# A gate load in two halves, and the first gate unit begun on the first of them

## The chip, the cores and the metric

The kernel runs on one core of one Trainium2 chip. The metric is the device time of one execution in microseconds (us). All runs that are compared here are, with the kernel before, run in the same rounds on the same chip. Engines are named as in the profile: PE is TensorE (matmuls), PEld its weight loads, DVE VectorE, ACT ScalarE, POOL GpSimd, SP the engine that issues most loads.

## The reference, cut to what matters

```python
xn = _layernorm(x, axis=-1, eps=1e-5)                # x: 2048 x 512, bf16
return x + _A_ref(xn, w_r, w_i) + _B_ref(xn, w_gate, w_up, w_down)
# _B_ref: h = gelu(xn @ w_gate) * (xn @ w_up);  h @ w_down      (w_gate, w_up: 512 x 1792)
# _A_ref: a 2-D real FFT of xn, a product with w_r + i w_i, and the inverse FFT
```

## The kernel before

The rows of x are taken as 16 "columns" of 128 rows. Columns 0 and 1 are normalised first and transposed by PE. Then gate and up products start while the rest of the weights comes in, in small units (a unit is the product of some columns with some weight columns). Everything is one fixed order of instructions per engine, made by a small scheduler from estimated times.

The parts that the change touches:

```python
    pin(load_x(0, 1))
    pin(load_x(1, 1))
    idx_t = pc.tile([P, 3], I32, name="idx_t")
    nc.sync.dma_start(out=idx_t[:], in_=...)          # 1.5 KB, used after 40 us
    load_w(Wg_sb, 0, 512)                             # 512 KB: all four contraction blocks e of gate columns 0..511
    load_w(Wu_sb, 0, 512)                             # 512 KB: the first up load
    load_x(2, 2)
    for e in range(0, NE, 2):
        load_w(Wg_sb, 512, 1024, e=slice(e, e + 2))
    load_w(Wu_sb, 512, 1024)                          # the second up load
    load_x(4, 4)
    load_w(Wg_sb, 1024, DF)
    load_w(Wu_sb, 1024, DF)
    load_x(8, 2)
    load_x(10, 2)
    # ... (cut)

    def spin_on():                                    # fillers that keep PE busy
        for k in range(11):
            nc.tensor.matmul(sp_ps[:, :P], lhsT=spin[:], rhs=x_t[:, 0, :P], start=True, stop=True)

        # ... (cut) first unit: column 0, gate columns 0..511
        if k == 0:
            g = add("PE", occ / 4, lambda: mm_part(0, 1), [xT_op[0, 0]], key=1000, acq=("G",), t_min=WG_LAND[0])
            between["t", 0].deps.append(g)            # column 1's transposes come behind this quarter
            g = add("PE", occ / 4, lambda: mm_part(1, 2), [g, between["t", 1]], key=1000.1)
            g = add("PE", occ / 2, lambda: mm_part(2, NE), [xT_op[0], g], key=1000.2, lat=occ / 2 + 0.3)
```

All these loads are issued by SP, one after the other. From the ninth load on, each waits for the landing of the one eight places before.

## Time and profile before

| kernel before | us |
|---|---|
| median of three runs (178.33 to 178.76) | 178.74 |
| span of the profiled run | 176.9 |
| first gate matmul | 6.66 |
| first up load: issued, landed, wanted by PE | 2.65, 8.05, 8.63 |
| second up load: issued, landed, wanted by PE | 4.89, 11.99, 12.69 |

"Landed" is the last of the 16 increments of a load's semaphore in the trace, "wanted" the first weight load that reads it. SP's timeline (start, length of the issuing instruction):

```profile
2.18 0.43 SPq L277 DMA_DIRECT2D Wg_sb<-in_B_w_gate_dram  x1
2.65 0.51 SPq L277 DMA_DIRECT2D Wu_sb<-in_B_w_up_dram  x1
```

And the table of stretches of one microsecond; its last two columns are the busy share of the DMA engines and GB/s:

```profile
4.00:5.00 1.00, 1.00 (x12) 0.91 (x9) 0.94 (x4) 0.30 (x1) 0.00 (x0) 1.00 0.92 280
5.00:6.00 1.00, 0.73 (x9) 0.38 (x8) 0.93 (x5) 0.29 (x1) 0.00 (x0) 1.00 1.10 378
6.00:7.00 1.00, 0.97 (x18) 0.80 (x16) 0.67 (x4) 0.00 (x0) 0.00 (x0) 1.00 1.07 378
```

From 5 to 7 us the DMA engines are busy throughout.

### The profile page before, as it was taken

The numbers are of one execution on the slowest core, as the hardware profiler recorded it, in microseconds if no ns is written. First come the engines' busy times: TensorE is split into PE (matmuls) and PEld (weight loads), VectorE is DVE, ScalarE is ACT, GpSimd is POOL, SyncE is SP. The second block draws the span as 40 slices with busy tenths as digits, with TensorE's granted clock in tenths as the row PEclk, the third lists the DMA queues.
The fourth block names the chain that finished last, engine by engine and source line by source line (L and its number), as shares of the span: only waits on it lengthen the run. The fifth ranks groups of instructions, "written<-read, shape, count | busy, mean of one in ns | idle before, by whom it ended". The sixth has DMA issues, their size and how long they took to land.

```text
span 176.9 us, 3143 instructions
## 1 busy us (share of the span) xinstructions
PE 172.8 (98%) x1150; PEld 96.9 (55%) x1150; DVE 115.9 (66%) x255; ACT 96.0 (54%) x171; POOL 17.2 (10%) x38
## 2 busy tenths in 40 slices
PE   7999999999999999999999999999999999999993
PEld 7798845455545554555555455454445445444463
DVE  2588999987434599979899999643516325345333
ACT  3452489799736988898899965362112111211200
POOL 1020340506760000000000000000000000000000
DMA  3999999233717802211201510200122221221212
GB/s 99 323 387 377 371 199 151 60 64 71 246 41 238 299 0 59 59 30 35 59 19 42 152 47 15 59 0 4 59 89 89 77 75 60 89 88 60 82 40 59
DMA packets 21743, 19.35 MB, mean 109 GB/s; under 512 B 8480, under 2 KB 20000, under 8 KB 21728
## 3 DMA queue, kind: packets, MB, share of 16 engines
q1 hardware_dynamic: 21312, 17.84, 36.4%
q0 software_dynamic: 416, 1.32, 2.6%
q8 instruction: 9, 0.15, 0.4%
q14 instruction: 6, 0.05, 0.1%
HBM read 13.38 MB, written 2.10 MB: 87 GB/s over the span
## 4 chain that ended last, share of the span: by engine, by line
PE 95%; DVE 2%; DMA 1%; issue 0%
PE u_ps L494 27%; PE y_ps L829 27%; PE g_ps L494 25%; PE g_ps L502 2%; PE bp L589 2%; PE yp L780 2%; PE gp L750 2%; PE dp L647 2%; PE y_ps L833 2%; PE ep L656 2%; DMA x_t<-in_A_x_dram 1%; DVE stats L339 1%; PE tp L351 1%; DVE xn L345 0%; DVE xnT L354 0%; DVE y_sb L836 0%
## 5 line engine op out<-in xcount | busy, mean ns | idle before, releaser
L494 PE MATMUL u_ps<-xnT,Wu_sb 128*128 128x512 bf16 (+2 forms) x272 | 57.1, 341 | 0.0
L494 PE MATMUL g_ps<-xnT,Wg_sb 128*128 128x512 bf16 (+1 forms) x224 | 53.3, 364 | 0.0
L829 PE MATMUL y_ps<-Wd_sb,hT 128*128 128x512 bf16 (+2 forms) x252 | 51.1, 355 | 0.0
L512 DVE TENSOR_TENSOR hT<-u_ps,ge 128x512 bf16<-128x512 f32 x56 | 38.4, 688 | 18.1 <-PE u_ps L494 16.5
L507 ACT ACTIVATE ge<-g_ps 128x512 bf16<-128x512 f32 x56 | 33.5, 601 | 22.3 <-PE g_ps L494 18.3
L494 PEld LDWEIGHTS <-Wu_sb 128*128 128x128 bf16 x272 | 24.8, 98 | 20.7
L829 PEld LDWEIGHTS <-hT 128*128 128x128 bf16 x252 | 23.2, 98 | 22.4
L494 PEld LDWEIGHTS <-Wg_sb 128*128 128x128 bf16 x224 | 21.5, 98 | 20.5
L786 ACT CAST yf<-yp 128x512 bf16<-128x512 f32 x16 | 9.3, 586 | 40.5 <-PE yp L780 40.5
L836 DVE TENSOR_TENSOR y_sb<-y_ps,y_sb 128x512 bf16<-128x512 f32 (+2 forms) x18 | 11.1, 632 | 30.0 <-PE y_ps L833 30.0
L661 ACT CAST E<-ep 64x512 bf16<-64x512 f32 x32 | 18.5, 579 | 1.4 <-PE ep L656 1.0
L339 DVE BATCH_NORM_STATS2 stats<-x_t 128x6 f32<-128x512 bf16 x16 | 10.4, 674 | 3.9 <-DMA x_t<-in_A_x_dram 3.9
L456 ACT ACTIVATE xn<-x_t,nb,rstd 128x512 bf16<-128x512 bf16 x12 | 9.5, 812 | 1.0 <-POOL nb L370 1.0
L559 ACT CAST ds<-dp 128x512 bf16<-128x512 f32 x16 | 9.2, 597 | 0.8 <-PE dp L647 0.8
L559 ACT CAST Gs<-gp 128x512 bf16<-128x512 f32 x16 | 8.7, 591 | 0.6 <-PE gp L750 0.5
L559 ACT CAST Bs<-bp 128x512 bf16<-128x512 f32 x16 | 8.3, 606 | 0.5 <-PE bp L589 0.5
L792 DVE TENSOR_TENSOR lv<-yf 128x512 bf16<-128x512 bf16 x16 | 6.1, 421 | 1.5 <-ACT yf L786 0.6
L780 PEld LDWEIGHTS <-Gs 128*128 128x128 bf16 x64 | 4.8, 98 | 3.5
L799 DVE TENSOR_TENSOR yt<-lv 128x512 bf16<-128x512 bf16 x16 | 6.1, 421 | 0.3
L833 PE MATMUL y_ps<-yt,RI_t 128*128 128x512 bf16 (+2 forms) x18 | 6.1, 355 | 0.0
L780 PE MATMUL yp<-CT,Gs 128*128 128x128 bf16 x64 | 6.0, 219 | 0.0
L571 DVE TENSOR_TENSOR A<-xn 128x1024 bf16<-128x1024 bf16 x8 | 5.2, 676 | 1.0 <-ACT xn L456 1.0
(65 smaller groups left out, 125.5 us busy)
## 6 DMA issues: line engine op xcount, KB each, us to landing
F<-F SPq DMA_DIRECT2D x32, 64.0 KB, 2.0
y_sb<-in_A_x_dram SPq DMA_DIRECT2D x16, 128.0 KB, 2.1
out_dram<-y_sb SPq DMA_DIRECT2D x15, 128.0 KB, 1.7
Wd_sb<-in_B_w_down_dram SPq DMA_DIRECT2D x1, 1792.0 KB, 7.6
x_t<-in_A_x_dram SPq DMA_DIRECT2D x5, 256.0 KB, 9.8
Wu_sb<-in_B_w_up_dram SPq DMA_DIRECT2D x2, 512.0 KB, 6.2
Wg_sb<-in_B_w_gate_dram SPq DMA_DIRECT2D x1, 768.0 KB, 10.2
Wu_sb<-in_B_w_up_dram SPq DMA_DIRECT2D x1, 768.0 KB
```

The source lines that it names most:

```text
L339: V.bn_stats(out=st[:], in_=x_t[:, c, :])
L456: xn_op[c] = add("ACT", 0.72, lambda c=c: A.activation(out=xn[:, c, :], in_=x_t[:, c, :], func=AF.Identity, bias=nb[:, c:c + 1], scale=rst ...
L494: T_.matmul(b[name][:, f], lhsT=W_[:, e, (f0 + f) * P:(f0 + f + 1) * P], rhs=rhs[:, e, :], start=(e == 0), stop=(e == NE - 1))
L507: A.activation(out=b["ge"][:], in_=b["g_ps"][:], func=AF.Gelu_apprx_tanh)
L512: V.tensor_tensor(out=hT_of(sb, f0, m, o, w), in0=b["u_ps"][:], in1=b["ge"][:], op=ALU.mult)
L559: A.copy(out=o, in_=i)
L661: A.copy(out=b["E"][64 * h:64 * h + 64, r], in_=b["ep", h][64 * r:64 * r + 64])
L780: T_.matmul(t[:, q], lhsT=late["G"][:, q, c0 + j], rhs=IQ[q], start=(q == 0), stop=(q == 3), skip_group_check=True)
L786: A.copy(out=b["yf"][:, j], in_=b[j][:])
L829: T_.matmul(b[o][:], lhsT=hT_of(sb, f, 1, cl * P, P)[:, 0], rhs=Wd_sb[:, f, o:o + w], start=(f == 0), stop=False)
L833: T_.matmul(b[o][:], lhsT=late["RI"][:, c, :], rhs=late["yt"][:, c, o:o + w], start=False, stop=True)
L836: V.tensor_tensor(out=b["y"][:, o:o + w], in0=b[o][:], in1=b["y"][:, o:o + w], op=ALU.add)
```

## The change

The intent: PE's first real work waits for the 512 KB gate load until 6.66, though column 0 is ready at 6.03. With the load in two contraction halves, the first gate matmuls can start on the first half. Fewer fillers are needed, and column 1 is transposed behind the third quarter. Columns 8 to 11 become one load, so that the number of loads stays the same.

```diff
-    load_w(Wg_sb, 0, 512)
+    for e in range(0, NE, 2):
+        load_w(Wg_sb, 0, 512, e=slice(e, e + 2))
...
-    load_x(8, 2)
-    load_x(10, 2)
+    load_x(8, 4)
...
-        for k in range(11):
+        for k in range(5):
...
-            g = add("PE", occ / 4, lambda: mm_part(0, 1), [xT_op[0, 0]], key=1000, acq=("G",), t_min=WG_LAND[0])
+            g = add("PE", occ / 2, lambda: mm_part(0, 2), [xT_op[0, 0]], key=1000, acq=("G",), t_min=5.5)
+            g = add("PE", occ / 4, lambda: mm_part(2, 3), [xT_op[0], g], key=1000.01, t_min=WG_LAND[0])
             between["t", 0].deps.append(g)
-            g = add("PE", occ / 4, lambda: mm_part(1, 2), [g, between["t", 1]], key=1000.1)
-            g = add("PE", occ / 2, lambda: mm_part(2, NE), [xT_op[0], g], key=1000.2, lat=occ / 2 + 0.3)
+            g = add("PE", occ / 4, lambda: mm_part(3, NE), [g, between["t", 1]], key=1000.2, lat=occ / 4 + 0.3)
```

The scheduler's order changes in one more place: four matmuls of the third unit's up product, which read the second up load, now stand ahead of the transposes of columns 2 and 3.

More of the change, by code (lines that the diff above doesn't have):

```diff
@@ L410, in first_two @@
         T(0, 1)
-        add("PE", 0.61, spin_on, [o["T", 0, 1]], key=-1500, lat=0.61, after=o["T", 0, 1])
+        add("PE", 0.28, spin_on, [o["T", 0, 1]], key=-1500, lat=0.28, after=o["T", 0, 1])
         table = add("ACT", 1.3, lambda: None, [o["root", 1]], key=-1500, lat=1.3)
```

## The prediction

> **What bounds the kernel now.** I read the page's busy shares and chain first, then TensorE's own waits over the whole run, then the chain and the weight-load timeline of the first 13 us, and last the DMA landings.
>
> From the page (engine shares, then the chain by engine):
> ```profile
> PE 172.8 (98%) x1150; PEld 96.9 (55%) x1150; DVE 115.9 (66%) x255; ACT 96.0 (54%) x171; POOL 17.2 (10%) x38
> ...
> PE 95%; DVE 2%; DMA 1%; issue 0%
> ```
> All waits of TensorE in the run (us in total, times, longest):
> ```profile
> PE sp_ps L320 <- DVE minus_half L266: 1.1, 1, 1.1
> PE tp L351 <- DVE xn L345: 0.2, 1, 0.2
> ```
> TensorE is the bound, and after its start it never waits. So the run is "the moment of the first real matmul" plus a fixed stream of matmuls plus the stores at the end. A change of the start can only pay what it moves that stream forward. The chain of the first microseconds (start, length, what) shows that moment:
> ```profile
> 5.74 0.29 DVE xnT L354
> 6.03 0.07 DVE rstd L399
> 6.10 0.25 DVE xnT L354
> 6.35 0.33 DVE xn L345
> 6.68 0.38 PE g_ps L502 x4
> 7.06 0.22 PE tp L351 x4
> 7.29 1.56 PE g_ps L502 x28
> ```
> and the weight-load timeline (start, length; it gives starts better than the matmul row, whose ends are modelled):
> ```profile
> 5.81 0.66 PEld L324 LDWEIGHTS <-spin 128*128 128x128 bf16 x11
> 6.66 0.23 PEld L502 LDWEIGHTS <-Wg_sb 128*128 128x128 bf16 x4 [0.20 <-DMA Wg_sb<-in_B_w_gate_dram]
> 6.84 0.27 PEld L351 LDWEIGHTS <-xn 128*128 128x128 bf16 x4
> 7.07 1.60 PEld L502 LDWEIGHTS <-Wg_sb 128*128 128x128 bf16 x28
> 8.63 1.83 PEld L494 LDWEIGHTS <-Wu_sb 128*128 128x128 bf16 x32
> 10.42 1.68 PEld L502 LDWEIGHTS <-Wg_sb 128*128 128x128 bf16 x16
> 12.19 0.55 PEld L351 LDWEIGHTS <-xn 128*128 128x128 bf16 x8
> 12.69 0.37 PEld L494 LDWEIGHTS <-Wu_sb 128*128 128x128 bf16 x4
> ```
> The reader is to see two things. Column 0's first half was transposed and copied at 6.03 (5.74 + 0.29), but the first gate matmul runs at 6.66, released by the gate weights; 11 filler matmuls (spin) bridge the time. And the transposes of column 1 (6.84) stand behind the first quarter only: three quarters (12 matmuls) then cover the copy of column 1 before the second unit needs it.
>
> **What the Trainium skill says.** "DMA: Bandwidth & Descriptors", Why a DMA increments its semaphore by 16 and not by 1: only the full 16 says that the data has landed. The trace agrees: the 16 increments of the 512 KB gate load, issued at 2.18, run from 5.53 to 6.62, and the matmul starts at 6.66. "Perfetto Trace Analysis", DMA Optimizations: "Splitting DMAs into smaller chunks may allow some to start sooner", above all where DMA engines are idle. Here they are only half busy (51%) from 3 to 4 us and full from 5 us on, so the first half can come sooner, but the sum of both cannot by much. "TensorE: Matmul & The Clock Gate", What's actually happening: the array runs at half rate until about 3.4 us of activity. The trace fits: the 37 first fillers take 3.87/37 = 105 ns each, the 11 later ones 0.66/11 = 60 ns. Same page, Back-to-back issue gap: some 81 ns a matmul sustained at N=128; the trace has 1.60/28 = 57 ns, and I use 57.
>
> **The change part by part.**
>
> *Split load.* One 512 KB issue becomes two of 256 KB. Issues cost some 0.45 us of the queue each, so the second half is issued at about 2.65, and the up weights, columns 2 and 3 and so on each about 0.5 later. The first half: later 256 KB gate halves land 0.77 apart (9.74 and 10.51), so on the slowest DMA engine it should be in some 0.75 before 6.62, at about 5.9 (estimate). The second half should land where the whole did, 6.6, perhaps 0.1 to 0.3 sooner[...].
>
> *Fewer fillers.* 5 instead of 11: 6 x 0.06 = 0.36 off; they end at 5.81 + 0.30 = 6.11, just where the first gate matmuls can start (copy done 6.03). Without this they would block until 6.47.
>
> *First half of the unit.* 8 matmuls, 8 x 0.057 = 0.46, from 6.11 to 6.57. This is a start 0.55 earlier than 6.66, and it is what the change aims at.
>
> *Third quarter, transposes, fourth quarter.* The third quarter needs the second load (6.62) and runs 6.66 to 6.89. The four transposes follow at 6.89 (column 1 is normalised by 6.67), against 6.84 before. So the transposes do not come earlier. The fourth quarter runs from 7.12 to 7.35.
>
> *The second unit* needs column 1's copy. Before, transposes began at 6.84, the copy ran 7.21 to 7.50: 0.66 from transpose to data, plus some 0.05 of release. Now this gives 6.89 + 0.71 = 7.60. TensorE has nothing else between 7.35 and 7.60: **about 0.25 us of the 0.55 comes back as a new wait**. Before, the second unit began at 7.07 + 12 x 0.057 = 7.75. So what is left is 7.75 - 7.60 = **0.15 us**; with a second half landing 0.1 to 0.2 sooner it could be 0.25 (the copy of the normalised column, 6.67, sets the limit).
>
> *Downstream.* The order of instructions shows one more move: four matmuls of the third unit's up product now stand before the transposes of columns 2 and 3. Before, transposes ran at 12.19 and these at 12.69, while their weights landed at 11.99; now TensorE wants them at about 12.19 - 0.15 - 0.1 = 11.95 to 12.05. So this load becomes just critical and caps the gain at about 0.13 to 0.2. The other loads have room: up weights land 8.05 (wanted about 8.5), gate 512 to 1023 at 9.74 and 10.51 (wanted about 10.25 and 10.7), columns 2 and 3 at 9.01 feed a VectorE chain that is unchanged.
>
> *Columns 8 to 11 as one load.* It keeps the number of loads in front of each semaphore reuse equal. Column 8 will be known landed only with 11, at 19.74 instead of 19.06, while VectorE wants it at 19.22: a VectorE stall of some 0.5. VectorE has slack again at 25.2, and an up unit's buffer is wanted back only two units (3.5 us) later, so I put 0 on the path.
>
> Sum: -0.15, capped to about -0.13, with some chance of -0.25. Against the 178.74 before (178.33 to 178.76, mean 178.61) this is under 0.15%.
>
> **Rivals.** (1) The whole 0.55 arrives at the end: 178.2. For it speaks that TensorE never waits later; against it the column 1 copy, which can't start before 6.67, and the up weights at 11.99. (2) A new wait eats everything: the second half lands 0.2 or more later, as its issue is 0.47 later, or the third unit's up weights land at 12.2 or later; each later tenth then costs a tenth: 178.7 to 179.0. For it: the load stands just at the edge. Against it: the queue issues about 512 KB per 0.5 us and the DMA moves that in 1.4 us, so it is issued well ahead. (3) VectorE's stall at column 8 pushes the units near 20 to 25 us: VectorE is full there (2.00 of 2.00 from 16 to 20), but a wait of TensorE would need a delay above some 0.7; no gain lost otherwise. (4) A longer filler gap lets the array slow down: only if the first half landed so late that TensorE idled for long; I give this 2%.
>
> **Range and chances.** The most likely gain is 0.13 to 0.2, so I predict 178.55. The three runs before spread over 0.43, more than the effect, so the range is mainly that: 178.2 to 178.9. Beyond 2% (3.6 us) neither way has a mechanism: nothing here removes or adds that much.
>
> **What would show it.** First gate matmuls at about 6.1 with no wait for weights, or a short one: step one right. Transposes of column 1 at 6.8 to 6.95, then 4 gate matmuls, then a TensorE idle of 0.2 to 0.3 that ends with the copy on VectorE: the give-back right; if there is none, or the transposes come at 6.6, I mis-sized it. The second unit at 7.5 to 7.65. A short wait near 12 us for the up weights: the cap right. VectorE waiting at some 19.2 to 19.7 for columns 8 to 11, with no TensorE idle behind it. The prediction fails if any TensorE idle over 0.3 shows after 8 us, or if the first half lands after 6.3.

## The result, and the profile after

The changed kernel takes 180.41 us (median of four runs, 179.70 to 181.01), the kernel before 178.59 (four runs, 178.33 to 178.76). The ratio is 1.0101, with a 95% interval of 1.0053 to 1.015. Ratios here are the mean time of one kernel's runs over that of the other's of the same rounds, so not quite the ratio of the medians quoted. It is slower by about 1%: within 2%, as foretold, but outside the predicted range.

All waits of PE in the changed kernel (us in total, times, longest):

```profile
PE u_ps L494 <- DMA Wu_sb<-in_B_w_up_dram: 1.3, 2, 1.0
PE sp_ps L320 <- DVE minus_half L266: 1.1, 1, 1.1
PE bp L589 <- ACT Bs L559: 0.3, 1, 0.3
```

The first line is new. The weight-load timeline shows where (start, length, then in brackets the idle time before it and what ended it):

```profile
5.43 0.32 PEld L324 LDWEIGHTS <-spin 128*128 128x128 bf16 x5
5.71 0.76 PEld L502 LDWEIGHTS <-Wg_sb 128*128 128x128 bf16 x12
6.42 0.27 PEld L351 LDWEIGHTS <-xn 128*128 128x128 bf16 x4
6.65 0.32 PEld L502 LDWEIGHTS <-Wg_sb 128*128 128x128 bf16 x5
7.14 0.88 PEld L502 LDWEIGHTS <-Wg_sb 128*128 128x128 bf16 x15 [0.17 <-issue]
9.16 1.79 PEld L494 LDWEIGHTS <-Wu_sb 128*128 128x128 bf16 x32 [1.14 <-DMA Wu_sb<-in_B_w_up_dram]
11.25 1.64 PEld L502 LDWEIGHTS <-Wg_sb 128*128 128x128 bf16 x16 [0.31 <-DMA Wg_sb<-in_B_w_gate_dram]
13.48 0.33 PEld L494 LDWEIGHTS <-Wu_sb 128*128 128x128 bf16 x4 [0.58 <-DMA Wu_sb<-in_B_w_up_dram]
```

The start is as intended, and better: the first gate matmul at 5.71 instead of 6.66. Then PE runs out of work. The up product starts at 9.16 instead of 8.63, and after the second up load's wait the stream is 1.2 us late (the next gate unit starts at 15.58 instead of 14.39). Both waits are for loads that had landed in time before. The first up load landed at 9.11 instead of 8.05, the second at 13.44 instead of 11.99. SP's timeline and the stretches say more:

```profile
2.18 0.94 SPq L277 DMA_DIRECT2D Wg_sb<-in_B_w_gate_dram  x2
3.16 0.47 SPq L277 DMA_DIRECT2D Wu_sb<-in_B_w_up_dram  x1
```

```profile
4.00:5.00 1.00, 1.00 (x12) 0.91 (x9) 0.96 (x5) 0.28 (x1) 0.00 (x0) 1.00 0.99 332
5.00:6.00 1.00, 1.00 (x15) 0.78 (x14) 0.83 (x6) 0.29 (x1) 0.00 (x0) 1.00 0.91 174
6.00:7.00 1.00, 1.00 (x20) 0.97 (x18) 0.54 (x3) 0.10 (x1) 0.00 (x0) 1.00 0.95 312
```

The DMA engines move more than before from 4 to 5 us (332 against 280 GB/s) and then fall to 174, although four further loads have been issued by then. The busy share stays at 0.91 because a few packets take long: of the 170 packets of 1 KB that start here, 18 took over 100 ns each and together half of the packet time (mean 85 ns against 48 in the kernel before, median 46 in both). The 204 GB/s missing in this microsecond, over some 375 GB/s, are 0.54 us of transfer.

That is not all of the lateness. Of the 16 increments of the first up load the eighth came 0.35 later than before (7.60 against 7.25) and the last 1.06 later (9.11 against 8.05). For the second up load it is 0.56 and 1.45. So the larger part is that the slowest DMA engine fell further behind the others.

### The profile page after: what moved, and what is told of

Same layout as the page of the kernel before. It is cut to its first block, busy times and chain, and to the rows that moved or that the text cites. A ratio compares the mean times of both kernels' runs of the same rounds, so it can differ in the third digit from the quotient of the medians.

```text
span 179.2 us, 3132 instructions
## 1 busy us (share of the span) xinstructions
PE 173.4 (97%) x1144; PEld 96.7 (54%) x1144; DVE 115.8 (65%) x255; ACT 96.0 (54%) x171; POOL 17.2 (10%) x38
## 4 chain that ended last, share of the span: by engine, by line
PE 75%; DMA 10%; ACT 5%; DVE 4%; issue 2%; SPq 1%; POOL 1%; ACTq 0%
PE y_ps L829 27%; PE u_ps L494 19%; PE g_ps L494 18%; DMA x_t<-in_A_x_dram 7%; DMA Wu_sb<-in_B_w_up_dram 3%; PE yp L780 2%; PE gp L750 2%; PE dp L647 2%; ACT Bs L559 2%; PE y_ps L833 2%; PE ep L656 2%; ACT ge L507 1%; ACT xn L456 1%; DVE stats L339 1%; DVE hT L512 1%
```

## The experiments

The theories. **Loads**: the new loads are late and make PE wait. **Order**: PE's new order itself costs. If it is the loads, why: **dry queue** (the up load is issued 0.5 later and its packets are not there when the gate packets end) or **halves** (half loads make the next load slow, whenever it is issued), or the **merged** load of columns 8 to 11.

### Loads or order

`e1`: the changed kernel unmodified, for a second profile.

> The changed kernel again, for a second profile. If the slow loads are the kernel's own doing: ratio about 1.01, first up weights landing near 9.1 us and the second up load near 13.4 again. If they were an accident of that run: up weights near 8.1 and 12.0, time 178.4 to 179.

Measured: 180.07 us (179.87 to 180.17), ratio 1.0088 (1.0067 to 1.0108). Up loads landed at 9.52 and 13.72. It is the kernel's own doing. In this profile the account is simple. Against the kernel before, PE is 0.73 early at its first gate matmul, 0.48 early at the second unit, 0.94 late at the up product, 1.10 late at the third gate unit, 1.48 late behind the second up load, and stays so to the end. In the first profile PE lost a further 1.1 between 23 and 43 us (1.19 late at 15.58, 2.28 late from 43 us on); that does not come back here.

`e2`: the old loads with the new order.

```diff
-    for e in range(0, NE, 2):
-        load_w(Wg_sb, 0, 512, e=slice(e, e + 2))
+    load_w(Wg_sb, 0, 512)
...
-    load_x(8, 4)
+    load_x(8, 2)
+    load_x(10, 2)
```

> Loads as before (one whole gate load, columns 8 to 11 in two), instruction order and 5 fillers as changed. Theory A (the split and merged loads make the later loads land late): this lands like before (8.05, 11.99) and takes 178.4 to 178.9. Theory B (the new TensorE order itself costs: column 1 behind the third quarter, up product ahead of the transposes): 179.5 to 181 as the changed kernel, with the landings of before.

Measured: 178.64 us, ratio 1.0009 (0.9990 to 1.0028), up loads at 8.36 and 11.95.

`e3`: the mirror image, the new loads with the old order and 11 fillers.

> Loads as changed, instruction order and 11 fillers as before. Theory A: slow like the changed kernel, 179.5 to 181, waits for the up weights at about 9 and 13 us. Theory B: 178.3 to 178.8, as before.

Measured: 180.35 us, ratio 1.0120 (1.0087 to 1.0153). Its weight loads:

```profile
6.59 0.44 PEld L502 LDWEIGHTS <-Wg_sb 128*128 128x128 bf16 x4
9.51 1.79 PEld L494 LDWEIGHTS <-Wu_sb 128*128 128x128 bf16 x32 [0.69 <-DMA Wu_sb<-in_B_w_up_dram]
```

The old order, started at the old time, loses as much. So the loads cost the time, and the order costs nothing.

`e4`: the changed kernel, with columns 8 to 11 in two loads again.

```diff
-    load_x(8, 4)
+    load_x(8, 2)
+    load_x(10, 2)
```

> The changed kernel with columns 8 to 11 in two loads again; the split stays. Theory A1 (the merged load stalls VectorE at 21.8 us and with it TensorE by 0.2 at 23.8 and 0.7 at 40 to 42): this gains 0.5 to 0.9 on the changed kernel, about 179.5 to 180, and the two late TensorE waits go. Theory A2 (all loads are late because the stream as a whole is late): no gain, the late waits stay.

Measured: 180.06 us, ratio 1.0098 (1.0058 to 1.0137), as `e1`. The merged load is not the cause. What is left is the split.

### Why the split makes the next load late

`e5`: the second gate half issued from ScalarE.

```diff
+    load_w(Wg_sb, 0, 512, e=slice(0, 2))
+    pin(load_w(Wg_sb, 0, 512, eng=nc.scalar, e=slice(2, 4)))
```

> The changed kernel, but the second gate half is issued from ScalarE, so that the first up load is issued at about 2.65 again instead of 3.16. Theory dry queue (the DMA engines finish the gate weights near 5.1 us and find too few descriptors of the up load, issued 0.5 later): no drop of the DMA rate from 5 to 6 us (over 330 GB/s instead of 174), up loads land near 8.1 and 12.1, time 178.2 to 178.8. Theory split itself (two half loads make the next one slow, whenever it is issued): up weights land after 9 and 13 us, time 179.7 to 180.5.

Measured: 180.31 us, ratio 1.0100; up loads at 8.52 and 12.77 in a profile of the fastest run (179.19). This test went wrong: the first up load was issued at 2.65 as meant, but ScalarE issued the load at 1.06, during its table load, ahead of what I meant, and column 1 landed at 4.50 instead of 3.70. So it does not decide between the two theories. The rate that the dry queue had foretold from 5 to 6 us (over 330 GB/s) did not come: it was 263.

`e6` and `e7`: the 1.5 KB index load moved behind the second up load, in the changed kernel and in the kernel before.

```diff
-    nc.sync.dma_start(out=idx_t[:], in_=...)         # ahead of the first gate load
...
+    nc.sync.dma_start(out=idx_t[:], in_=...)         # ahead of load_x(4, 4)
```

> The changed kernel with the small index load (1.5 KB) moved behind the second up load, so every weight load is issued 0.45 earlier, but with the same distance between them. Dry queue: the drop stays but comes 0.4 earlier, up loads near 8.6 and 13.0, time about 179.6. Split itself: the same. If the 128 packets of 12 B of the index load had held the queue up, more: up loads near 8.1, time 178.3 to 178.8.

Measured: 179.30 us, ratio 1.0043 (0.9993 to 1.0093); up loads at 9.23 and 13.15, and the rate falls near 4.8 us. As foretold: all is earlier, the fall stays.

> The kernel before with the index load moved in the same way, no split. Control for the last one and a candidate: weights land 0.4 earlier (gate 6.2), first gate matmul at 6.2, but column 1's transposes still wait for 6.7: gain 0.1 to 0.2, 178.4 to 178.6.

Measured: 178.46 us, ratio 0.9993 (0.9953 to 1.0033); gate at 5.80, up loads at 7.27 and 11.34, no fall. The gain is too small to be told from none.

`e8`: the kernel before with one unused 1.5 KB load between gate and up.

```diff
     load_w(Wg_sb, 0, 512)
+    idx2_t = pc.tile([P, 3], I32, name="idx2_t")
+    nc.sync.dma_start(out=idx2_t[:], in_=...)
     load_w(Wu_sb, 0, 512)
```

> The kernel before with one more small load (1.5 KB, unused) between the gate and the up load: issue of the up load 0.47 later as in the changed kernel, without a split. Dry queue: partly slow, as the gate weights end later here: up loads near 8.3 to 8.8 and 12.2 to 12.9, time 178.6 to 179.4. Split itself: as before, 8.1 and 12.0, 178.4 to 178.8.

Measured: 179.55 us (178.73 to 180.54), ratio 1.0054 (0.9994 to 1.0114). First up load at 7.64, no fall behind the gate packets; but a deeper one from 7 to 8 us (241 GB/s against 270), and the second up load at 12.65. Undecided: the first landing speaks for halves, the second for the dry queue. The stretches behind the gate packets, with the up load issued at 3.20, as late as in the changed kernel (3.16):

```profile
5.00:6.00 1.00, 1.00 (x11) 0.82 (x10) 0.82 (x6) 0.29 (x1) 0.00 (x0) 1.00 1.10 362
6.00:7.00 1.00, 1.00 (x20) 1.00 (x18) 0.40 (x3) 0.00 (x0) 0.00 (x0) 1.00 1.12 353
```

`e10`: in the kernel before, the third gate load (issued at 6 us, when megabytes are queued) in halves instead of the first.

```diff
-    load_w(Wg_sb, 1024, DF)
+    for e in range(0, NE, 2):
+        load_w(Wg_sb, 1024, DF, e=slice(e, e + 2))
```

> The kernel before with the third gate load (columns 1024 on, 768 KB, issued at 6 us, when the queue holds much) in two halves instead of the first. Dry queue: a split costs nothing where work is queued, DMA rate from 13 to 18 us stays 370 to 385 GB/s, the second half lands at 16.3 and the up load behind it at 18.4 as before (within 0.3). Split itself: these come 0.5 to 1 later.

Measured: the second half at 16.64, the up load behind it at 18.71, 0.35 and 0.33 later than before. The first gate load, which is not changed, was already 0.5 later in this run (7.13), and with it the start of PE (ratio 1.0028, two runs). The rate while the halves come, in this kernel and in the kernel before:

```profile
14.00:16.00 2.00, 2.00 (x20) 1.80 (x19) 1.50 (x3) 0.06 (x2) 0.00 (x0) 1.00 1.06 375
```

```profile
14.00:16.00 2.00, 2.00 (x21) 1.80 (x19) 1.82 (x4) 0.43 (x1) 0.00 (x0) 1.00 1.06 374
```

In this one profile, two halves cost no bandwidth where work is queued.

`e11`: the first gate load in quarters.

```diff
-    for e in range(0, NE, 2):
-        load_w(Wg_sb, 0, 512, e=slice(e, e + 2))
+    for e in range(NE):
+        load_w(Wg_sb, 0, 512, e=slice(e, e + 1))
```

> The changed kernel with the first gate load in four quarters of 128 KB: the dose doubled and more, two further issues ahead of the up load. Both theories: later still. Dry queue in numbers: each further issue costs about 0.5, so the up load lands near 10 and the second near 14.4, and the run takes about 181. If the lateness came from the engines meeting the up weights all at once (not from the number of issues), it stays at 9.1 and 13.4, 180.

Measured: up loads at 8.53 and 12.60, 179.94 us, ratio 1.0075. A miss: I had taken the loss as 0.5 per issue. The eighth of the 16 increments of the first up load does come later with each step (7.25 whole, 7.60 halves, 7.89 quarters), but the slowest DMA engine, which is what PE waits for, was less far behind here.

`e12`: the changed kernel with the second gate load (columns 512 to 1023) whole.

```diff
-    for e in range(0, NE, 2):
-        load_w(Wg_sb, 512, 1024, e=slice(e, e + 2))
+    load_w(Wg_sb, 512, 1024)
```

> The changed kernel with the second gate load (columns 512 to 1023) whole instead of in halves: one issue fewer ahead of the second up load, the first split stays. Dry queue: the first up load is late as in the changed kernel (about 9.1), the second up load comes 0.4 to 0.8 earlier (12.6 to 13.0 instead of 13.4), time 179.2 to 179.7. If only the first split counts: second up load 13.4, 180.

Measured: up loads at 9.60 and 13.61, 180.35 us, ratio 1.0104 (1.0077 to 1.0130). A miss too: the second up load was issued half a microsecond earlier than in the changed kernel and came no earlier. So the loss is made once, behind the first gate load, and the later loads carry it on.

`e13`: the kernel before with two unused 1.5 KB loads between the whole gate load and the up load. No split, only a later issue.

> The kernel before with two small unused loads between the whole gate load and the up load, which is then issued at about 3.7. Late issue theory: the gate packets end at about 5.4, 1.7 after the up load's issue, so the rate falls to under 250 KB in the microsecond behind them and the first up load lands after 8.8. Halves theory: the rate holds at over 330 KB a microsecond until 6.5, the up load lands at 7.6 to 8.2.

Measured: 180.66 us (two runs), ratio 1.0116 (1.0087 to 1.0146), up loads at 8.81 and 13.59. SP's timeline, then the stretches:

```profile
2.65 0.50 SPq L287 DMA_DIRECT2D idx_t<-spec_rows  x1
3.20 0.43 SPq L289 DMA_DIRECT2D idx_t<-spec_rows  x1
3.67 0.43 SPq L277 DMA_DIRECT2D Wu_sb<-in_B_w_up_dram  x1
```

```profile
5.00:6.00 1.00, 0.67 (x10) 0.49 (x10) 0.94 (x6) 0.29 (x1) 0.00 (x0) 1.00 0.99 251
6.00:7.00 1.00, 0.76 (x15) 0.59 (x12) 0.56 (x2) 0.00 (x0) 0.00 (x0) 1.00 0.77 234
```

The fall from 378 GB/s is here without a first gate load in halves, and with it a loss as large as the changed kernel's. The packets of the small loads are too short to make it: 256 of them, 9 ns each, are 0.14 us on each of 16 DMA engines. So a late issue alone can make such a fall and such a loss. Two things keep this from settling the changed kernel. The up load is issued 1.02 later here, and only 0.51 later there; with 0.55 (`e8`) there was no fall behind the gate packets. And PE waits elsewhere: hardly for the first up load (8.85 instead of 8.63), but 0.77 for a gate load and 0.76 for the normalised columns 2 and 3.

`e14`: the changed kernel, cut into one quarter and three quarters.

```diff
-    for e in range(0, NE, 2):
-        load_w(Wg_sb, 0, 512, e=slice(e, e + 2))
+    load_w(Wg_sb, 0, 512, e=slice(0, 1))
+    load_w(Wg_sb, 0, 512, e=slice(1, 4))
```

> The changed kernel with the gate load cut into one quarter and three quarters. Late issue: as the changed kernel, up load issued at 3.16, rate falls near 5.1, first up load near 9, 180. Halves: the large second part acts like a whole load, rate holds, up load near 8.2.

Measured: 178.70 us in both runs, ratio 1.0006 (0.9977 to 1.0036), up loads at 8.39 and 12.29, and no fall:

```profile
5.00:6.00 1.00, 1.00 (x12) 0.86 (x11) 0.78 (x5) 0.29 (x1) 0.00 (x0) 1.00 1.12 367
6.00:7.00 1.00, 1.00 (x13) 1.00 (x12) 0.32 (x1) 0.00 (x0) 0.00 (x0) 1.00 1.01 354
```

The up load is issued at 3.13 here, as in the changed kernel. By my expectation that was the halves theory's case. But the gate packets also end later than with halves in the changed kernel's first profile (5.38 against 5.08; in `e1` they end at 5.38 too, and the rate falls). So I looked at the distance between the two in every run.

`e16`: the kernel before with the first up load in halves.

> The kernel before with the first up load in two halves, gate whole. Late issue: the rate holds to about 6.5, as the up halves are issued early enough, then falls deeper behind them, as columns 2 and 3 are issued 0.5 later: these land near 9.5, second up load near 12.6. Halves: the same or worse; the rate falls already where the second half begins, near 6.2.

Measured: 179.38 us, ratio 1.0045 (1.0013 to 1.0076). The rate holds to 6.5 us and falls deeper after 7.5; columns 2 and 3 land at 9.26 (9.01 before), the second up load at 12.34 (11.99). The dry queue's picture, in a weaker form.

### All runs in one table

"Gate end" is the time at which 720 of the first 768 KB (columns 0 and 1 and the gate load) had started, from the packets of the trace. "Distance" is from the issue of the first up load to the gate end. "KB next" is what starts in the microsecond behind it. `e5` is left out, as it uses two queues (it has a distance of 3.38 and only 270 KB behind it); so is the first up load of `e16`, which comes in two. `e15` is the second run of the kernel of `e9`, below.

| run | first gate load | up issued | gate end | distance | KB next | first up load: 8th, last increment | second up load landed | ratio |
|---|---|---|---|---|---|---|---|---|
| e2 | whole | 2.65 | 5.48 | 2.83 | 370 | 7.36, 8.36 | 11.95 | 1.0009 |
| e7 | whole | 2.18 | 4.97 | 2.79 | 366 | 7.00, 7.27 | 11.34 | 0.9993 |
| e10 | whole | 2.65 | 5.42 | 2.77 | 377 | 7.28, 8.46 | 12.14 | 1.0028 |
| e15 | whole | 2.18 | 4.94 | 2.76 | 356 | 6.99, 7.45 | 11.54 | 0.9980 |
| e9 | whole | 2.18 | 4.88 | 2.70 | 369 | 6.94, 7.13 | 11.42 | 0.9977 |
| before | whole | 2.65 | 5.33 | 2.68 | 368 | 7.25, 8.05 | 11.99 | 1 |
| e16 | whole | 2.65 | 5.29 | 2.64 | 364 | in two | 12.34 | 1.0045 |
| e14 | 1 + 3 quarters | 3.13 | 5.38 | 2.25 | 335 | 7.34, 8.39 | 12.29 | 1.0006 |
| e1 | halves | 3.17 | 5.38 | 2.21 | 229 | 7.51, 9.52 | 13.72 | 1.0088 |
| e8 | whole | 3.20 | 5.32 | 2.12 | 355 | 7.42, 7.64 | 12.65 | 1.0054 |
| e6 | halves | 2.69 | 4.73 | 2.04 | 221 | 6.96, 9.23 | 13.15 | 1.0043 |
| e12 | halves | 3.17 | 5.12 | 1.96 | 157 | 7.69, 9.60 | 13.61 | 1.0104 |
| after | halves | 3.16 | 5.08 | 1.92 | 157 | 7.60, 9.11 | 13.44 | 1.0101 |
| e4 | halves | 3.17 | 5.06 | 1.90 | 170 | 7.53, 9.23 | 13.27 | 1.0098 |
| e3 | halves | 3.16 | 5.05 | 1.89 | 160 | 7.64, 9.47 | 13.41 | 1.0120 |
| e13 | whole | 3.67 | 5.37 | 1.69 | 183 | 8.12, 8.81 | 13.59 | 1.0116 |
| e11 | quarters | 4.07 | 5.41 | 1.33 | 172 | 7.89, 8.53 | 12.60 | 1.0075 |

From a distance of 2.25 up, 335 KB or more follow; from 2.04 down, at most 221. Between them two runs stand the wrong way round (2.21 with 229, 2.12 with 355), so the distance sorts the runs well but not perfectly. Halves shorten the distance from both sides: the up load is issued 0.5 later, and, `e1` apart, the gate packets end some 0.25 earlier.

The landing of the first up load, for which PE waits, is sorted better by halves than by distance. All six runs with halves land it between 9.11 and 9.60, with the last increment 1.51 to 2.27 behind the eighth; no other run of the table lands it later than 8.81 or has more than 1.18 between the two. Against the kernel before, `e8` (one more issue, no split) and `e14` (an uneven split) lose 0.66 and 0.30 at the second up load, the runs with halves 1.28 to 1.73 (`e6`, against `e7`, 1.81). Nor does this prove the halves guilty: in `e13`, without them, columns 2 and 3 have such a gap (8.82 to 10.64). The limit near 2.2 was read out of these runs after the fact, and no run was foretold from it; a usable run with halves and an up load issued early is missing. So it is shown that the first gate load's split makes the next loads late, and that a later issue alone can do so. How much of the changed kernel's loss is the later issue, and how much the halves themselves, is not shown.

### A version that beats both

`e9`: what the change wanted, without the split. The gate load is whole, the index load is moved behind the second up load (which brings every weight load 0.47 forward without a further issue), and PE's order and fillers are the changed ones.

> A candidate: whole gate load and columns 8 to 11 in two as before, index load behind the second up load, TensorE order and 5 fillers as changed. With the loads of the control before (gate 5.8, up 7.3 and 11.3) and no split: first gate matmul at about 6.1, third quarter ahead of the transposes of 6.7, second unit some 0.15 earlier than in that control; up loads ready in time. 178.1 to 178.5. If the new order itself costs, 178.6 or more.

Measured: 178.10 us (177.92 to 178.37), ratio 0.9977 (0.9952 to 1.0001). Its weight loads:

```profile
5.69 0.71 PEld L502 LDWEIGHTS <-Wg_sb 128*128 128x128 bf16 x12
6.36 0.26 PEld L351 LDWEIGHTS <-xn 128*128 128x128 bf16 x4
7.90 1.83 PEld L494 LDWEIGHTS <-Wu_sb 128*128 128x128 bf16 x32
```

The same early start as in the changed kernel, and the up product follows at 7.90 without a wait. Part of the start is luck: column 0 landed at 3.01 here.

> The candidate (whole gate load, index load later, TensorE order as changed) with five rounds: 178.0 to 178.3 against 178.5, ratio 0.997 to 0.999, interval clear of 1.

`e15`, five rounds of the same kernel, measured: 178.24 us (178.10 to 178.61), ratio 0.9980 (0.9961 to 0.9998). It is faster than the kernel before by 0.2%, and than the changed kernel by 1.2% (178.24 over 180.41, medians of different rounds). Its kept profile is of the slowest of the six runs (178.61): column 0 landed at 3.34, the first gate matmul came at 6.29, and PE's stream ends level with that of the kernel before. So the 0.2% rests on the times alone.

## Why the prediction was right or wrong

**What bounds the kernel: right.** PE's stream sets the end. What delays it early is carried to the end unchanged, in `e1` 1.48 of 1.48.

**First gate matmul at 6.1 without a wait for weights: right in kind.** It came at 5.71 and 5.93. Column 0 landed at 3.02 and 3.25 in these runs, 3.40 in the profile before, and the first half landed at 5.36 and 5.68, sooner than my 5.9. Part of this is luck: the loads of column 0 are the same in all these kernels, and came 0.15 to 0.38 sooner here.

**The transposes keep their time: wrong by some tenths.** They moved to 6.42 and 6.60 (I had 6.89), as the second half landed at 6.04 and 6.36 instead of 6.62.

**The new wait for column 1's copy: right.** It was 0.17 (I had 0.25). The second unit started at 7.14 and 7.31, 0.65 and 0.48 earlier than before; the promise was 0.15. Up to here the change pays more than I said.

**"The other loads have room: up weights land 8.05 (wanted about 8.5)": this step failed.** I took the landings of the kernel before as given. The up weights landed 1.06 and 1.47 later, the second up load 1.45 and 1.73 later; columns 2 and 3, which I had left at 9.01, landed at 10.43 and 10.73. The prediction had this in part as its rival 2 (the second up load at 12.2 or later), with the right sign, sized it up to 179.0 and argued against it: "the queue issues about 512 KB per 0.5 us and the DMA moves that in 1.4 us, so it is issued well ahead". That counts bytes issued. The runs showed in its place that the up load, issued at 3.16, did not follow the gate packets at full rate when they ended at 5.08: the rate fell from 332 to 174 GB/s, the eighth increment came 0.35 later and the slowest DMA engine 1.06 later. That the split loads do this, and not PE's order or the merged load, is shown by `e2`, `e3` and `e4`. `e13` shows that a later issue alone, of twice the size, can cost as much; the shares of issue and halves here stay open. The Trainium skill's advice that I quoted ("Perfetto Trace Analysis", DMA Optimizations) did hold for the half itself, which came sooner; I did not ask who stood behind it in the queue.

**The cap near 12 us: right in place, wrong in size.** The second up load did become critical, with waits of 0.58 and 0.60; I had it at the edge with 0.

**Columns 8 to 11 in one load: right on the average, not in each run.** VectorE waited 1.33 for them in the first profile. PE lost 1.1 behind that between 23 and 43 us, which I had put at 0; the second profile has no such loss, and `e4` gains nothing by undoing the merge.

The sum was -0.13 and became +1.8 by the medians. The term that was mis-sized is the landing of the up loads: 0 in my sum; in `e1` it turns a lead of 0.48 into a lag of 1.48.

What stays open: what happens between an issue and its first packets, which the trace does not show; why the last increment of the first up load is 1.5 us or more behind the eighth in all six runs with halves and 0.6 with quarters; and what halves cost beyond the shorter distance.

## What to carry to other kernels

Before a load is split at the start of a kernel, look at the load behind it: here the DMA rate fell for a microsecond behind the halves, the slowest DMA engine fell further behind, and the slack of the next loads (0.6 to 0.7 us) was gone. Where the queue is deep, as for the third gate load here, the same split cost no bandwidth. The cheaper way to an earlier start was to move a load that nobody needs yet out of the way.

## What the Trainium skill lacked or had wrong

- "DMA: Bandwidth & Descriptors", Latency and other measured facts, gives about 600 ns to the first byte for loads from SP, and does not say from where it counts. In the profile before, the first packet starts at 1.82, 1.02 us after its load's issue begins (0.80) and 0.63 after it ends (1.19): counted from the end the figure agrees.
- No page says how early the next load has to be issued for the rate to hold. Behind the first gate load it held (335 KB or more in the next microsecond) in all eight runs of the table with a distance of 2.25 us or more, and fell in eight of nine with less. That is no rule for other places: in the kernel before it also falls, to 270 GB/s, from 7 to 8 us, although the next load had been issued at 3.20.
- "Perfetto Trace Analysis", DMA Optimizations, says that splitting may let some transfers start sooner. The first half landed 1.26 sooner than the whole (5.36 against 6.62), but no page says that the load behind a split one can land later by as much: 1.06 to 1.47 here.
- "TensorE: Matmul & The Clock Gate", Back-to-back issue gap, gives some 81 ns a matmul for a sustained stream at N=128; the stream here runs at 57 ns.
- No page says how much the landing of one load varies from run to run. The same 512 KB gate load, issued at 2.17 or 2.18 behind the same loads, landed between 6.15 and 7.13 in six profiles (before 6.62, e2 6.97, e8 6.15, e10 7.13, e13 6.72, e16 6.89), with the slowest DMA engine setting the time.
